# The projections of three head pairs written as one burst each instead of two, with neighbouring operations in another order

## The chip, the cores and the metric

The kernel runs on one core of a Trainium2 chip. The metric is device time in microseconds (us); lower is better. PE is TensorE (matrix multiplies), DVE is VectorE, ACT is ScalarE, POOL is GpSimd, SP is SyncE, which issues the DMAs. "Bank" means a PSUM bank, the 128 x 512 float tile into which matmuls write.

## What is computed

An attention with exponential features over 8 batches and 8 heads of 576 positions and 64 dimensions, and behind it a gated product over the 4608 x 512 result. q, k, v and all weights are drawn at random.

```python
def phi(x):                      # for q and for k, omega is 128 x 64
    proj = np.einsum('bhsd,md->bhsm', x, omega)
    sq = np.sum(x * x, axis=-1, keepdims=True) / 2.0
    h = proj - sq
    h = h - np.max(h, axis=-1, keepdims=True)
    return np.exp(h) / np.sqrt(m)
kv = np.einsum('bhsm,bhsd->bhmd', k_p, v)
z = np.sum(k_p, axis=2)
num = np.einsum('bhsm,bhmd->bhsd', q_p, kv)
den = np.einsum('bhsm,bhm->bhs', q_p, z)[..., None] + 1e-06
x = (num / den)                  # laid out as 4608 x 512
a = x @ w_a                      # 512 x 1536
b = x @ w_b
return (a * b) @ w_out           # 1536 x 512
```

## The kernel before

The work is cut into blocks of 512 rows of x, one batch each (the last 64 positions of all batches make a ninth block). For each block, the attention of four pairs of heads is computed while the PE does the gated product of an earlier block. So PE holds two kinds of work in one stream: the products `pa`, `pb` (x by w_a and w_b, L1307) and `o` (by w_out, L1120), each an instruction group of three 128x512 matmuls (from block 2 on, x by w_a and w_b is done in another form, L1405), and between them the attention of pairs that come later.

The attention of a pair begins with the projection: 64 x 64 matmuls that multiply X (k and q of the pair, eight chunks of 128 positions) by omega into the banks `ppk` and `ppq`. From these, ACT copies the scores into `hk` and `hq` (L396), DVE takes the maximum of each row (a reduce) and works out the bias of the exponentials (two small instructions), and ACT computes the exponentials in place. Then PE multiplies `hk` with v into `pkv` (L906).

Two routines write that projection. `four` (L576) does four chunks into two banks of the ring `at` and is called twice per pair; its scores are handled in `scores` (L632; reduces at L659, biases at L666 and L667, exponentials at L680). `eight` (L593) does all eight chunks in one burst of 64 matmuls (L607) into four banks: two of the ring `at` (`ppk`, `ppq`) and, if it is called with an empty `room`, two of the ring `ab` (`ppkb`, `ppqb`), whose two banks otherwise hold `pa` and `pb`. Its reduces are 1024 wide (L617), its biases stand at L622 and L623, its exponentials at L627. Copies come first on the banks of the second half.

A bank of `ab` that holds `pa` is free when ACT has copied it (a<-pa, L396), one with `pb` when DVE has multiplied it with that copy (a<-pb,a at L1315). The next `pa` or `pb` needs a free bank, and so does `eight`.

Which routine a pair takes is decided in `moe_block`, which starts each step of the gated product with `begin([] if len(steps) >= CFG["OWN"] else None)` (L1294): pairs that start at step 16 or later go to `eight`. The four pairs of the third block (u = 8, 9, 10, 11 in the numbering of `shifted`, L800; their tiles are called `_2_0` to `_2_3`) start at steps 8, 11, 14 and 17, so before the change the first three take `four` twice and the fourth takes `eight`.

Nothing is scheduled at run time. A frozen table, `ORDER`, lists every operation of the program by number; `Graph.plan` replays it, with `SLOTS` (which buffer of its ring each tile takes) and `ENGS` (which of two engines does an operation that either could do). Each engine runs its instructions in that order and waits by semaphores for what they read and for buffers that come free.

In the first 40 us there is hardly any gated product to work on. Block 0's pairs (tiles `_0_0` to `_0_3`) are projected and normalised there, weights are split into two float32r parts, tails of 64 positions (`sme`, `htk`, `htq`, `x32t`, `tails`) are handled, and the squares of k and q (`nat`, on POOL at L750 or ACT at L749) are summed by DVE into `sq` (L752).

Of the kernel before, what the change touches and what calls it, by code (L numbers as in the profile page):

```python
# [40 lines left out]
CFG = dict(EFIRST=0, HALF=1, IDSP=1, EDF=("DVE", "ACT", "POOL"), ROUNDS=2, ZS=800, ZB=(300, 1600, 3600), ZD=(300, 1600, 3100), HQ=(1100, 2600, 3600), BACK2=(300, 1100, 2600), TW=(), XL=["v0", "v1", "Xt0", "ht2", "hq0"], OWR=["raw0", "raw1"], ONE=((7, 1),), SAFE=500, OWN=16, OWNU=(), TG=1, G4=4, WAIT=150, RAW=600, FAST=(0, 1, 2, 3), JOIN0=False, WARM=7, HROOM=["w0", "u1", "w1", "u2", "w2", "u3"], H=3, TURN=(7,), BACK=1500, AT=2, GATES=(-4, -1, 2, 5), SQPE=4, MARGIN=1200, LOAD=1100, SUMS=1000, NATS=(1, 2, 3), CONV=(28000, 2600))  # L41
# [152 lines left out]
"""  # L194

SLOTS = dict(
# [1435 lines left out]
```

## Time and profile before

| what | value |
| --- | --- |
| median of 3 runs | 1031.36 us (1030.74 to 1031.38) |
| the profiled execution | 1031.69 us, of which the span is 1029.7 us |
| PE busy | 1021.7 us, 99% of the span, 9963 matmuls |
| DVE busy | 789.8 us, 77% |
| ACT busy | 637.8 us, 62% |
| POOL busy | 110.8 us, 11% |
| main DMA queue | 87.6% of 16 engines' span |

The span runs from the first to the last instruction of the core; the remaining 2.0 us of the execution lie around it. A matmul's duration overlaps with that of the next, so on PE the distance between the starts of two instructions tells how long one takes, and the end in the row does not. In a timeline a row starts at the first column's time (us from the span's start), and xN counts instructions that were put into one row.

### The profile page before, as it was taken

What the parts mean: (1) busy time and instruction counts of PE and PEld (TensorE: products, weight loads), DVE (VectorE), ACT (ScalarE), POOL (GpSimd) and SP (SyncE); (2) the same over time, 40 slices, a digit from 0 to 9 for tenths busy, and PEclk for the clock granted to TensorE, in tenths of its full rate; (3) what the DMA queues carried; (4) which work ended last, traced back from release to release, by engine and by line L of the source; (5) the groups of instructions that cost most, each with busy time, mean ns of one, the idle gap of its engine ahead of it and who ended that gap; (6) DMA issues with size and microseconds to landing.
All of it is one profiled execution on the core that took longest, in us unless ns stands there. A gap on an engine that the chain in (4) does not pass through costs nothing.

```text
span 1029.7 us, 25658 instructions
## 1 busy us (share of the span) xinstructions
PE 1021.7 (99%) x9963; PEld 900.4 (87%) x9963; DVE 789.8 (77%) x1561; ACT 637.8 (62%) x1688; POOL 110.8 (11%) x182
## 2 busy tenths in 40 slices
PE   9999999999999999999999999999999999999998
PEld 7777777778788889888889988888888999999998
DVE  7999999999987877776767767687756467877555
ACT  7999998776676666675666556675654134344322
POOL 2012111210111111111110011111110000000000
PEclk9999999999999999999999999999999999999999
DMA  9787888998999999989898998989797888989981
GB/s 355 244 308 255 274 257 281 328 320 285 338 338 321 340 350 333 341 299 324 286 341 306 325 290 284 350 273 320 242 331 244 307 281 329 366 319 346 358 310 60
DMA packets 122185, 312.95 MB, mean 304 GB/s; under 512 B 17488, under 2 KB 39120, under 8 KB 122064
## 3 DMA queue, kind: packets, MB, share of 16 engines
q1 hardware_dynamic: 121600, 310.72, 87.6%
q8 instruction: 79, 1.29, 0.5%
q10 hardware_dynamic: 464, 0.59, 0.2%
q14 instruction: 42, 0.34, 0.1%
HBM read 254.74 MB, written 56.52 MB: 302 GB/s over the span
## 4 chain that ended last, share of the span: by engine, by line
PE 96%; DVE 3%; ACT 0%; issue 0%; DVEq 0%; ACTq 0%
PE p L1405 41%; PE o L1120 23%; PE pb L1307 6%; PE pa L1307 6%; PE o_P L1190 5%; PE pkv L906 3%; PE pm L977 2%; PE ppk L607 2%; PE ppk L587 2%; PE p L607 1%; PE p L1190 1%; DVE sm L659 1%; PE ppke L587 1%; DVE raw L456 0%; PE none L426 0%; DVE sq L752 0%
## 5 line engine op out<-in xcount | busy, mean ns | idle before, releaser
L1120 PE MATMUL o<-wo,ghl 128*128 128x512 f32 x1008 | 269.6, 397 | 0.0
L1120 PEld LDWEIGHTS o<-wo,ghl 128*128 128x128 f32 x1008 | 178.6, 188 | 35.5 <-issue 4.3
L396 ACT COPY c<-p 128x512 f32<-128x512 f32 x150 | 87.5, 583 | 182.0 <-PE p L1405 174.4
L1417 DVE TENSOR_TENSOR c<-p,c 128x512 f32<-128x512 f32 x144 | 98.7, 685 | 63.8 <-PE p L1405 36.5
L1405 PE MATMUL p<-Sa,t 128*128 128x256 f32 x1008 | 133.9, 282 | 0.0
L1405 PEld LDWEIGHTS p<-Sa,t 128*128 128x128 f32 x1008 | 126.9, 190 | 2.4 <-issue 0.3
L859 POOL TENSOR_TENSOR z<-hk 128x256 f32<-128x256 f32 x54 | 47.2, 873 | 610.5 <-ACT hk L627 356.1
L1481 DVE TENSOR_TENSOR c<-c 128x512 f32<-128x512 f32 x82 | 56.7, 696 | 46.3 <-ACT c L396 45.7
L1307 PE MATMUL pa<-x,wa 128*128 128x512 f32 x288 | 79.6, 400 | 0.0
L941 ACT ACTIVATE hq<-hq,dn 128x128 f32<-128x128 f32 x216 | 70.5, 393 | 11.9 <-DVE dn L937 11.5
L1307 PE MATMUL pb<-x,wb 128*128 128x512 f32 x288 | 77.8, 397 | 0.0
L1405 PE MATMUL p<-x,wb 128*128 128x256 f32 x504 | 73.5, 281 | 0.0
L1405 PE MATMUL p<-x,wa 128*128 128x256 f32 x504 | 73.4, 281 | 0.0
L1405 PEld LDWEIGHTS p<-x,wa 128*128 128x128 f32 x504 | 67.7, 189 | 2.9
L1405 PE MATMUL p<-Sb,bq 128*128 128x256 f32 x504 | 67.7, 283 | 0.0
L1405 PE MATMUL p<-x,t 128*128 128x256 f32 x504 | 67.5, 282 | 0.0
L1405 PEld LDWEIGHTS p<-Sb,bq 128*128 128x128 f32 x504 | 64.9, 189 | 2.9
L1405 PEld LDWEIGHTS p<-x,t 128*128 128x128 f32 x504 | 64.7, 189 | 2.9
L1405 PE MATMUL p<-Sb,t 128*128 128x256 f32 x504 | 67.0, 282 | 0.0
L1405 PEld LDWEIGHTS p<-x,wb 128*128 128x128 f32 x504 | 65.6, 189 | 0.1
L1405 PEld LDWEIGHTS p<-Sb,t 128*128 128x128 f32 x504 | 63.4, 189 | 1.4 <-ACT c L396 0.5
L1307 PEld LDWEIGHTS pb<-x,wb 128*128 128x128 f32 x288 | 53.3, 188 | 12.7 <-issue 0.9
(225 smaller groups left out, 1969.2 us busy)
## 6 DMA issues: line engine op xcount, KB each, us to landing
t<-td SPq DMA_DIRECT2D x168, 512.0 KB
wo<-wod SPq DMA_DIRECT2D x96, 512.0 KB
bq<-bd SPq DMA_DIRECT2D x84, 256.0 KB
qdr<-qd SPq DMA_DIRECT2D x108, 160.0 KB
hq<-qdr SPq DMA_DIRECT2D x27, 640.0 KB
X<-in_kqt_dram SPq DMA_DIRECT2D x30, 512.0 KB
raw<-in_wab_dram SPq DMA_DIRECT2D x24, 512.0 KB
td<-ts SPq DMA_DIRECT2D x24, 512.0 KB
```

What stands on the lines that cost most here:

```text
L396: nc.scalar.copy(o(), i())
L587: nc.tensor.matmul(pps[w].ap[half, c * M:c * M + M], x()[rows, c * P + D * t:c * P + D * t + D], mo.ap[rows], start=True, stop=True)
L607: nc.tensor.matmul(flat[c // 4][w]()[half, c % 4 * M:c % 4 * M + M], x()[rows, c * P + D * t:c * P + D * t + D], om.ap[rows], start=True, ...
L859: g.op({"POOL": pool2(n)}, lambda e: nc.gpsimd.tensor_tensor(o(), a(), c(), op=ALU.add), r=r, w=w, alloc=list(al), prio=pri, deps=zload[-1 ...
L906: nc.tensor.matmul(pkv.ap[D * j + d:D * j + d + Q, 0:M], vb.ap[:, vc, d:d + Q], c(), start=(n == 0), stop=(n == 4))
L941: g.op({"ACT": 392}, lambda e, c=c, src=src: nc.scalar.activation(hq.ap[:, c], src(), AF.Copy, scale=dn.ap[:, c:c + 1]), r=[sd, (dn, None) ...
L1120: nc.tensor.matmul(po.ap[:], ghl.ap[:, gi, t * P:(t + 1) * P], wo.ap[:, wi], start=(n == 0 and i == 0), stop=(n == NF - 1 and i == 2))
L1190: nc.tensor.matmul(pb.ap[:, t], A[0](ai)[:, t * P:(t + 1) * P], W[0](wi), start=begin and t == j == 0, stop=stop and j == 2 and (t == 1 or ...
L1307: nc.tensor.matmul(pb.ap[:], wt.ap[:, wi, c], xs[c].at(xi), start=(c == 0 and i == 0), stop=(c == NC4 - 1 and i == 2))
L1405: nc.tensor.matmul(pb.ap[:, w], W[w][0](wi, c), X[0](xi, c), start=fresh and n == w == 0, stop=n == 5, skip_group_check=True)
L1417: g.op({"DVE": dve(SM)}, lambda e: nc.vector.tensor_tensor(o.ap[:, q], pb.ap[:], C[y[0]].ap[:, y[1]], op=ALU.add), r=[(pb, 0), (pb, 1), (C ...
L1481: g.op({"DVE": dve(SM)}, lambda e, c=C[k]: nc.vector.tensor_tensor(c.ap[:, :, 1], c.ap[:, :, 1], c.ap[:, :, 0], op=ALU.mult), r=part, w=pa ...
```

## The change

`OWN` goes from 16 to 8, so that the pairs u = 8, 9 and 10 are also projected by `eight` with banks of their own. The graph then has four operations fewer for each of these pairs (5255 instead of 5267 in all), and `ORDER` and `SLOTS` are new tables for it; one letter of `ENGS` differs, by which one copy of an output tile goes from DVE to ACT. The number of PE instructions is the same, and so is SP's stream with its DMAs. DVE has 13 instructions fewer (four for each pair, two reduces of 1024 for four of 512 and two bias instructions for four, and the copy), ACT one more. Rows of the changed kernel carry a line number smaller by one, since a table is one line shorter.

```diff
 CFG = dict(
...
-OWN=16,
+OWN=8,
...
 ORDER = """
-    6 7 3 238 239 9 240 306 307 8 2 360 1 0 241 243 361 242 257 414 311 415 271 256 246 22 245 244 260 258 10 247 259 308 312 250 249 251 261 248 309 264 270 268 314 269 263
...
 SLOTS = dict(
...
-    tst="010212020132a323a93ba323",
+    tst="102012020132a323a93ba323",
...
 ENGS = (
-    "DDDDDDADADADDAADDDPPADDAPADAPPDDADAAAADDDDDADAAAADDADDAADADDAADADADDADDAADDDAADADADDADAADDAAAADADDDDDADADDDAAADADDDDAADDDDDDAAAD")
+    "DDDDDDADADADDAADDDPPADDAPADAPPDDADAAAADDDDAADAAAADDADDAADADDAADADADDADDAADDDAADADADDADAADDAAAADADDDDDADADDDAAADADDDDAADDDDDDAAAD")
```

PE's order is the same up to row 496 of 3137 and again from about row 776; between them the three pairs and the products around them stand differently. On PE at the first of the three pairs (u = 8; `pa0_10` and `pb0_10` are the products of step 10, `o0_2` and the like the output products), before:

```order
L1307 MATMUL pa0_10_2261<-x_0_2_826,wa10_2088 128x512 x3
L587 MATMUL ppk_2_00_2371<-om_67,X_2_0_2208 64x128
...
L587 MATMUL ppq_2_00_2372<-om_67,X_2_0_2208 64x128
L1307 MATMUL pa0_10_2261<-x_0_3_912,wa10_2088 128x512 x3
L1120 MATMUL o0_3_1120<-wo9_2213,ghl0_9_2366 128x512 x3
L1120 MATMUL o0_0_1124<-wo9_2213,ghl0_9_2366 128x512 x3
L1307 MATMUL pb0_10_2340<-x_0_1_734,wb10_2164 128x512 x3
L587 MATMUL ppk_2_04_2433<-om_67,X_2_0_2208 64x128
...
L587 MATMUL ppq_2_04_2434<-om_67,X_2_0_2208 64x128
L1307 MATMUL pb0_10_2340<-x_0_2_826,wb10_2164 128x512 x3
```

and after:

```order
L1306 MATMUL pb0_10_2259<-x_0_3_920,wb10_2192 128x512 x3
L1119 MATMUL o0_2_1205<-wo9_2159,ghl0_9_2339 128x512 x3
L1119 MATMUL o0_0_1114<-wo8_1893,ghl0_8_2162 128x512 x3
L606 MATMUL ppk_2_0_2388<-om_67,X_2_0_2225 64x128
...
L606 MATMUL ppq_2_0_2389<-om_67,X_2_0_2225 64x128
L606 MATMUL ppkb_2_0_2390<-om_67,X_2_0_2225 64x128
...
L606 MATMUL ppqb_2_0_2391<-om_67,X_2_0_2225 64x128
L1119 MATMUL o0_1_1122<-wo8_1893,ghl0_8_2162 128x512 x3
L1119 MATMUL o0_0_1114<-wo9_2159,ghl0_9_2339 128x512 x3
L1306 MATMUL pa0_11_2450<-x_0_0_722,wa11_2365 128x512 x3
```

The two bursts have become one, behind both products of step 10 and two groups of `o`, and two groups of `o` stand between the burst and the next `pa`.

On DVE at the same place, before (`hk`, `hq` are the scores of the pair):

```order
L948 STREAM_TRANSPOSE qd_2182<-hq_1_3_2036 128x4x288
...
L404 TENSOR_TENSOR ghl0_9_2366<-a0_9_2167,ghl0_9_2366 128x512
...
L659 TENSOR_REDUCE sm_2_0_2375<-hk_2_1_2373 128x4
L659 TENSOR_REDUCE sm_2_0_2375<-hq_2_0_2374 128x4
L666 SCALAR_TENSOR_TENSOR sm_2_0_2375<-sm_2_0_2375,sq_2_0_2101 128x2x4
...
L1315 TENSOR_TENSOR a0_10_2262<-pb0_10_2340,a0_10_2262 128x512
L659 TENSOR_REDUCE sm_2_0_2375<-hq_2_0_2374 128x4
```

and after:

```order
L947 STREAM_TRANSPOSE qd_2190<-hq_1_3_2040 128x4x288
L1314 TENSOR_TENSOR a0_10_2275<-pb0_10_2259,a0_10_2275 128x512
...
L616 TENSOR_REDUCE sm_2_0_2394<-hq_2_0_2393 128x8
L616 TENSOR_REDUCE sm_2_0_2394<-hk_2_1_2392 128x8
L621 SCALAR_TENSOR_TENSOR sm_2_0_2394<-sm_2_0_2394,sq_2_0_2114 128x16
```

The multiplication that frees the bank of `pb0_10` now stands right behind the transpose of the pair before, and ahead of both reduces.

On DVE in the first 20 us, before (`sme`: the tails of block 0; `sq_0_1`: the squares of pair 1, summed from `nat_0_1`, which POOL has squared):

```order
L659 TENSOR_REDUCE sme_0_0_273<-ppqe_0_00_270 128x4
L666 SCALAR_TENSOR_TENSOR sme_0_0_273<-sme_0_0_273,pse_0_00_296 128x8
L667 SCALAR_TENSOR_TENSOR sme_0_0_273<-pse_0_00_296,sme_0_0_273 128x8
L752 TENSOR_REDUCE sq_0_1_340<-nat_0_1_148 128x16
L659 TENSOR_REDUCE sm_0_1_244<-ppk_0_14_317 128x4
```

and after:

```order
L658 TENSOR_REDUCE sme_0_0_273<-ppqe_0_00_270 128x4
L751 TENSOR_REDUCE sq_0_1_339<-nat_0_1_151 128x16
L665 SCALAR_TENSOR_TENSOR sme_0_0_273<-sme_0_0_273,pse_0_00_297 128x8
L666 SCALAR_TENSOR_TENSOR sme_0_0_273<-pse_0_00_297,sme_0_0_273 128x8
L658 TENSOR_REDUCE sm_0_1_243<-ppk_0_14_319 128x4
```

The sum of the squares has gone ahead of the two bias instructions of the tails. Further on in the first 60 us, a few neighbours are exchanged on DVE and ACT: two copies `qT_0_1` (L398) go between the reduces of pair 3 and its two bias instructions, and the steps that split the weight tiles `raw1` and `raw2` (L452, L454) go ahead of the copy `x_0_2` on ACT.

## Rows read from the trace of the kernel before

**Rows 1.** The page: busy time by engine, granted clock in 40 slices, chain.

```profile
PE 1021.7 (99%) x9963; PEld 900.4 (87%) x9963; DVE 789.8 (77%) x1561; ACT 637.8 (62%) x1688; POOL 110.8 (11%) x182
PEclk9999999999999999999999999999999999999999
PE 96%; DVE 3%; ACT 0%; issue 0%; DVEq 0%; ACTq 0%
```

**Rows 2.** Waits of PE in the whole span: engine, line, releaser, us, times, longest.

```profile
PE none L426 <- PEq L1616: 0.8, 1, 0.8
...
PE px L1073 <- DVE x32t L1062: 0.4, 1, 0.4
```

**Rows 3.** Busy time in two stretches of 20 us, every engine, granted clock.

```profile
20.00:40.00 20.00, 18.91 (x400) 16.01 (x396) 19.39 (x60) 18.14 (x55) 0.73 (x4) 1.00 0.85 317
...
140.00:160.00 20.00, 20.00 (x188) 15.39 (x187) 17.57 (x36) 19.76 (x55) 2.52 (x4) 1.00 0.76 243
```

**Rows 4.** Timeline of PE around a call of four for u = 9: start, length, instruction.

```profile
167.13 0.84 PE L1307 MATMUL pa<-x,wa 128*128 128x512 f32 x3
167.90 0.32 PE L587 MATMUL ppk<-om,X 64*64 64x128 f32 x1
...
168.94 0.98 PE L1307 MATMUL pb<-x,wb 128*128 128x512 f32 x3
169.75 0.86 PE L1307 MATMUL pa<-x,wa 128*128 128x512 f32 x3
170.45 0.40 PE L1307 MATMUL pb<-x,wb 128*128 128x512 f32 x1
```

**Rows 5.** Timeline of PE around the call of eight for u = 11.

```profile
216.42 0.32 PE L607 MATMUL ppk<-om,X 64*64 64x128 f32 x1
...
217.24 0.27 PE L607 MATMUL ppk<-om,X 64*64 64x128 f32 x1
...
217.35 0.27 PE L607 MATMUL ppkb<-om,X 64*64 64x128 f32 x1
...
218.33 1.68 PE L1120 MATMUL o<-wo,ghl 128*128 128x512 f32 x6
```

**Rows 6.** Timeline of DVE in the first 40 us.

```profile
11.94 0.16 DVE L666 SCALAR_TENSOR_TENSOR sme<-sme,pse 128x8 f32<-128x8 f32 x1
...
12.22 1.22 DVE L752 TENSOR_REDUCE sq<-nat 128x16 f32<-128x1024 f32 x1
13.35 0.68 DVE L659 TENSOR_REDUCE sm<-ppk 128x4 f32<-128x512 f32 x1
...
39.75 0.42 DVE L1062 TENSOR_TENSOR x32t<-pn,rd 128x256 f32<-128x256 f32 x1
```

**Rows 7.** Timelines of POOL and of ACT there, with idle time and its releaser.

```profile
10.01 2.04 POOL L750 TENSOR_TENSOR nat<-nat 128x512 f32<-128x512 f32 x2 [4.88 <-DMA nat<-in_kqn_dram]
...
12.40 0.69 ACT L680 ACTIVATE htk<-ppke,sme 128x128 f32<-128x128 f32 x2
...
15.68 1.40 ACT L680 ACTIVATE hq<-ppq,sm 128x128 f32<-128x128 f32 x5 [0.38 <-DVE sm L673]
...
20.31 0.89 ACT L680 ACTIVATE hq<-ppq,sm 128x128 f32<-128x128 f32 x3 [0.39 <-DVE sm L673]
```

**Rows 8.** Timelines of DVE and ACT around the eight of u = 11.

```profile
213.04 1.38 DVE L948 STREAM_TRANSPOSE qd<-hq 128x1152 f32<-128x1152 f32 x1
...
215.23 0.69 DVE L1315 TENSOR_TENSOR a<-pb,a 128x512 f32<-128x512 f32 x1
...
218.45 0.59 ACT L396 COPY hk<-ppkb 128x512 f32<-128x512 f32 x1 [0.23 <-PE ppqb L607]
...
229.14 0.40 ACT L627 ACTIVATE hk<-hk,sm 128x128 f32<-128x128 f32 x1
```

**Rows 9.** The reduces of both forms: count, ns min/median/max, first and last start.

```profile
L617 DVE TENSOR_REDUCE sm<-hk x20: 1207/1219/1222, 219.1 to 756.1; 128x8 f32<-128x1024 f32 x20
...
L659 DVE TENSOR_REDUCE sm<-hk x6: 676/678/686, 150.3 to 198.6; 128x4 f32<-128x512 f32 x6
```

More of the change, by code (lines that the diff above doesn't have):

```diff
@@ L39 @@
 NS = 2
-CFG = dict(EFIRST=0, HALF=1, IDSP=1, EDF=("DVE", "ACT", "POOL"), ROUNDS=2, ZS=800, ZB=(300, 1600, 3600), ZD=(300, 1600, 3100), HQ=(1100, 2600, 3600), BACK2=(300, 1100, 2600), TW=(), XL=["v0", "v1", "Xt0", "ht2", "hq0"], OWR=["raw0", "raw1"], ONE=((7, 1),), SAFE=500, OWN=16, OWNU=(), TG=1, G4=4, WAIT=150, RAW=600, FAST=(0, 1, 2, 3), JOIN0=False, WARM=7, HROOM=["w0", "u1", "w1", "u2", "w2", "u3"], H=3, TURN=(7,), BACK=1500, AT=2, GATES=(-4, -1, 2, 5), SQPE=4, MARGIN=1200, LOAD=1100, SUMS=1000, NATS=(1, 2, 3), CONV=(28000, 2600))
+CFG = dict(EFIRST=0, HALF=1, IDSP=1, EDF=("DVE", "ACT", "POOL"), ROUNDS=2, ZS=800, ZB=(300, 1600, 3600), ZD=(300, 1600, 3100), HQ=(1100, 2600, 3600), BACK2=(300, 1100, 2600), TW=(), XL=["v0", "v1", "Xt0", "ht2", "hq0"], OWR=["raw0", "raw1"], ONE=((7, 1),), SAFE=500, OWN=8, OWNU=(), TG=1, G4=4, WAIT=150, RAW=600, FAST=(0, 1, 2, 3), JOIN0=False, WARM=7, HROOM=["w0", "u1", "w1", "u2", "w2", "u3"], H=3, TURN=(7,), BACK=1500, AT=2, GATES=(-4, -1, 2, 5), SQPE=4, MARGIN=1200, LOAD=1100, SUMS=1000, NATS=(1, 2, 3), CONV=(28000, 2600))
 ORDER = """
[149 rows of a table removed]
[148 rows of a table added]
 """
@@ L197 @@
     at=(
-        "0123456705613412652106537451673260731742751346507163014510110101010101101010100101011010101001010101101001010101010101010101010110101010101010101010101010010101"
-        "01010101010101010101010101010101010101010101"),
+        "0123456705613412652106537451673260731742751346507163014510110101010101101010100101011001101001101010010101010101010101010110101010101010101010101010010101010101"
+        "01010101010101010101010101010101010101"),
     Xw="01235a",
@@ L208 @@
     ht="0120120120120120",
-    sq="012012102101210210210120121021012012102",
+    tails="00000",
+    sq="012012102101201210210120121021012012102",
     qd="01010000000000000000000000000000",
@@ L212 @@
     nat="010101010101010011010110010011010101010101010101010101010101010",
-    tails="00000",
     rd="1010010101",
@@ L221 @@
     x="01230123012301230110",
-    ab="01010101010101010101010101010101010101010101010101011001",
+    ab="01010101010101010101100101010101010101100101010101010101011001",
     a="101010101010101010101010",
@@ L227 @@
     ghl="010101010101010101010101010101010101010101010101010101010101010101010101010101010101010101010101010101010101",
-    o="0321132032103210321032103210453210241350",
+    o="0321302132103210321032103210453210241350",
     z2="000000000000000000000000000",
@@ L236 @@
     kl="000000000000000000000000000",
-    tst="010212020132a323a93ba323",
+    tst="102012020132a323a93ba323",
     osb="10001010101010",
+    xa="01230123012301",
     t=(
@@ L241 @@
         "12340123"),
-    xa="01230123012301",
     st="00101010101010",
```

296 rows, old and new, of the table ORDER are left out of this document.

## The prediction

> **What bounds the kernel now.** I read the page first. PE is busy 99% of the span, the chain of what ended last lies on PE for 96% and on DVE for 3%, and the granted clock is at its highest digit in every slice [rows 1]. So the kernel takes as long as PE's stream of instructions, and a change can move the time in three ways: PE's instructions take less time, PE waits longer somewhere, or PE waits less. The second view, PE's waits over the whole span, shows how little the third can give: seven waits, the longest 0.8 us [rows 2]. The busy time in stretches tells where they lie: PE is busy 18.91 of the 20 us from 20 to 40, where DVE has 19.39, and 20.00 of 20 between 140 and 160 [rows 3]. So in the first 40 us DVE's row of instructions sets the end, and from there on PE does. The last of these waits, at 40 us, is for the DVE row x32t at 39.75 [rows 2, 6]. What DVE or ACT save behind 60 us is worth nothing by itself; what they cost there is worth nothing until it makes PE wait.
>
> The burst itself is read from PE's timeline by distances between starts. Around a call of four, a plain group of three products takes 0.70 us (169.75 to 170.45). From 167.13 to 169.75 stand one group, the burst of four chunks and one more group: 2.62 us [rows 4]. In steady state one chunk takes 0.11 us (217.24 to 217.35) [rows 5], so four chunks with two halves each make 8 x 0.11 = 0.88, and two plain groups 1.40. What is left, 2.62 - 1.40 - 0.88 = 0.34 us, is the price of going from full matmuls to 64 x 64 ones and back. Within an eight nothing is paid in the middle: its first half takes 0.93 us (216.42 to 217.35), its second 0.98 [rows 5], together 1.91, which is 16 x 0.11 and 0.15 of such edges.
>
> **The change part by part.** *One burst instead of two.* Each of the three pairs goes into and out of the 64 x 64 form once instead of twice: 0.34 us saved for each, 3 x 0.34 = 1.0 us, all of it on PE, which sets the end. Bounds: 0, if a longer burst pays elsewhere what it saves at its edges, and 1.1 (0.36 a pair, if the last digit of each row falls in its favour). I take 1.0, since an eight of this kernel was measured.
>
> *DVE has four instructions fewer for each pair.* Two reduces of 1024 at 1.22 stand for four of 512 at 0.68 [rows 9]: 2.72 - 2.44 = 0.28 us, and of the bias instructions one pair of 0.28 (11.94 to 12.22) [rows 6] is gone. It is 0.5 us a pair of heads, of an engine that PE does not wait for there [rows 2, 3]: worth nothing. The same goes for the copy that moves from DVE to ACT.
>
> *The first 20 us of DVE.* Here DVE sets the end, so an exchange of neighbours counts. The sum sq_0_1 goes ahead of the two bias instructions of the tails. In before it started at 12.22, when POOL's squares had been finished (10.01 + 2.04 = 12.05) for 0.17 us [rows 6, 7]; now it must wait for them. It then starts at about 12.1, and takes its 1.13 us (12.22 to 13.35); the biases, 0.28 (11.94 to 12.22), end at about 13.5 instead of 12.22, and the next reduce starts at about 13.5 where it was 13.35: DVE is later by 0.16. The larger part is ACT's. Its exponentials of the tails, which began at 12.40, begin 1.3 us later. ACT has two places with nothing to do behind that, 0.38 us at 15.68 and 0.39 at 20.31 [rows 7], which swallow 0.77; 0.53 us are left over. ACT hands back the banks whose scores DVE reduces next, so some of that reaches DVE. Against it stands the other exchange: with the copies between them, the two bias instructions of pair 3 no longer follow each other at once. A dependent pair of this kind takes 0.28 us for two short instructions [rows 6]; I put down 0.13 for the gap that closes. Net +0.4 (0.53 - 0.13). Bounds: -0.13, if nothing of ACT's delay arrives, and +1.3, if all of it does. I take +0.4, nearest to the row with the idle time that ACT has. Of the exchanged weight steps on ACT nothing is on the path: PE's last wait in this stretch is for DVE.
>
> *The middle, 145 to 210 us.* PE has no idle time there, so a gain is excluded; a loss is a new wait at one of three points. First, the second half of eight needs the bank of pb0_10, that is the end of the multiplication. From the last matmul of pb0_10 to the second half stand two groups of o (1.40) and the first half (0.93): 2.3 us. At u = 11 the multiplication started at 215.23 and took 0.69, and the second half began at 217.35 [rows 5, 8]: 1.4 us to spare. Second, pa0_11 follows two groups (1.40) behind the end of eight and needs the bank of ppkb copied by ACT; at u = 11 this copy started 0.12 us behind the end of the burst (218.33) and took 0.59 [rows 5, 8]: 0.7 to spare. At u = 8 ACT is fuller (19.76 of 20 us) [rows 3], so less. Third, pkv needs the exponentials of hk. In the changed order 17 groups stand between eight and pkv, 17 x 0.70 and the burst of 1.91 plus edges: 14.0 us. At u = 11 the last exponential of hk ended 229.14 + 0.40 - 216.42 = 13.1 us behind the start of the burst [rows 5, 8]: 0.9 to spare, again with an ACT that had less to do. I take +0.1 for all three pairs; bounds 0 and 1.5 (0.5 for each pair: one transpose of 1.4 more ahead, less the 0.9 that u = 11 had to spare).
>
> *The sum.* -1.0 + 0.4 + 0.1 = -0.5 us. On the profiled execution, 1031.69, that is 1031.2; the profiled one is 0.33 above the median of 1031.36, so on the median it is 1030.9. SP's stream is unchanged, so its queue moves with the buffers, by less than a microsecond.
>
> A measurement of this kernel can tell about 0.2% from no change, 2.06 us: 1029.3 to 1033.4 is "the same".
>
> **The rivals.** *The start loses all.* If the delay of 1.3 us on ACT reaches DVE whole, the sum is -1.0 + 1.3 + 0.1 = +0.4: 1031.8. For it: DVE has no gap there (19.39 of 20). Against: the two idle places on ACT [rows 3, 7]. Chance 0.17.
>
> *The bank of pb holds the burst up (slower).* In the changed order the multiplication stands right behind the transpose of qd, which took 1.38 us at u = 11 [rows 8] and itself reads what ACT finishes last for the pair before. From the point where the multiplication ends later than 2.3 us after pb's last matmul, every microsecond is one of PE. At u = 11 it ended at 215.92, 1.4 us ahead of the second half [rows 5, 8], so one such transpose ahead uses that up and no more; a transpose that itself waits as long again for ACT makes 1.38 us a pair. If all three pairs pay it, 4.1 - 1.0 + 0.4 = +3.5: 1034.9; if one does, +0.8: 1032.2. For it: the order on DVE. Against: only u = 8 has this neighbourhood for certain. Chance of all three 0.04, of one 0.10.
>
> *The copies are the bound.* A burst fills four banks that ACT alone empties, 0.59 us each [rows 8]; if other work of ACT stands between these copies, pa0_11 waits. At u = 8 ACT's stream from its copy of pa0_10 to that of ppkb has six long instructions and three short ones, some 4 us at 0.59 for a long one, where PE has four groups, the burst and two groups (4 x 0.70 + 1.91 + 1.40 = 6.1) between the two points. It decides from where ACT runs more than 2 us behind PE; what ACT had to spare at u = 11, 0.7 a pair, is the price if it is lost twice over, 2.1 in all, and 2.1 - 1.0 + 0.4 = +1.5: 1032.9. The Trainium skill ("TensorEngine Tiling (Array Packing)", PSUM Bottleneck) states this as the rule: tiling speeds up TensorE but not the emptying of PSUM, so the copy may become the bottleneck; it advises to share the copies between ScalarE and VectorE, which this kernel does not do for these banks. By that rule the time would be the 1032.9 of this rival. The trace so far disagrees, with 0.7 us to spare at u = 11. Chance 0.09.
>
> *The burst does not do what it says.* If the edges of a burst are paid for its length, the 1.0 is not saved: +0.5, 1031.9. The timeline of u = 11 speaks against it [rows 5]. Chance 0.05.
>
> **How the numbers follow.** The forecast, 1030.9, with a start between -0.13 and +0.8, has 0.55: 1030.2 to 1031.3. The cases up to 1032.9 have 0.17, 0.10, 0.09 and 0.05, the slow one 0.04. A range from 1030.0 to 1032.6 leaves out less than 2 in 10: the slow case and most of the copies' case above, and a few in a hundred below. Faster by over 0.2% would need 1029.3, more than twice what the burst gives: 0.03. Slower by over 0.2%: the slow case, and what a row of mishaps adds: 0.07. The same: 0.90.
>
> **What would show it.** The changed profile should have no 64 x 64 burst of 16 pairs of matmuls for u = 8 to 10, three more bursts with a 0.11 step into ppkb, and edges of 0.15 and not twice that. PE's total of waits should stay below 4 us, all of it before 60 us; the x32t that PE waits for at 40 us should come 0.2 to 0.8 later than 39.75. Step one is wrong if a burst has a gap between its halves. The middle is wrong if a wait of PE appears on ppkb behind a multiplication, on pa behind a copy, or on pkv behind an exponential. The forecast as a whole is wrong if the start moves by more than 1 us in either direction.

## The result: 1.3% slower, with the profile after

The changed kernel takes 1046.17 us (median of 6 runs, 1041.29 to 1048.18) against 1031.37 us of the kernel before beside it, 14.8 us more. The ratio estimated from all runs is 1.0132, 95% interval 1.012 to 1.0143 (the medians alone give 1.014). The forecast had been 1030.9, with a range up to 1032.6. The profiled execution took 1042.26 us, with a span of 1040.4.

The page after: busy time, and the chain that ended last.

```profile
PE 1020.7 (98%) x9963; PEld 899.5 (86%) x9963; DVE 786.6 (76%) x1548; ACT 638.1 (61%) x1689; POOL 109.0 (10%) x182
...
PE 75%; DVE 0%; ACT 0%; issue 0%
```

PE is busy 1.0 us less than before [rows 1], which is the saving that the edges of the bursts should give, and the span is 10.7 us longer. So the loss is waiting. PE's waits in the whole span after (us in total, times, longest):

```profile
PE pa L1306 <- ACT hk L395: 3.5, 2, 2.5
PE pkv L905 <- ACT hk L626: 2.9, 2, 1.7
PE pm L976 <- ACT kl L395: 1.4, 1, 1.4
...
PE px L1072 <- DVE x32t L1061: 0.8, 1, 0.8
```

The first three kinds were not there before [rows 2]. Stretches of 20 us after (length, then busy time of PE, PEld, DVE, ACT and POOL, clock, DMA share, GB/s) show where they lie:

```profile
20.00:40.00 20.00, 18.51 (x390) 15.61 (x388) 19.04 (x59) 19.41 (x58) 0.60 (x3) 1.00 0.85 318
...
140.00:160.00 20.00, 19.04 (x210) 14.63 (x210) 15.95 (x29) 16.63 (x42) 3.04 (x4) 1.00 0.70 256
...
220.00:240.00 20.00, 17.46 (x157) 13.62 (x156) 16.98 (x33) 13.81 (x37) 0.16 (x1) 1.00 0.90 323
```

Before, PE had no idle moment from 140 to 260 us ([rows 3] has the first 20 of them); now it is idle for 8.4 of these 120 us. ACT and DVE are busy for less of them as well (90 and 103 us, before 96 and 110). A row of PE that is the same in both traces comes 1.4 us later at 63 to 131 us and 10.6 us later at 244 us; behind that the distance stays between 10.0 and 10.6. The timeline of PE after, with the first burst and the waits:

```profile
152.04 0.32 PE L606 MATMUL ppk<-om,X 64*64 64x128 f32 x1
...
152.96 0.27 PE L606 MATMUL ppkb<-om,X 64*64 64x128 f32 x1
...
153.94 1.67 PE L1119 MATMUL o<-wo,ghl 128*128 128x512 f32 x6
156.57 1.65 PE L1306 MATMUL pa<-x,wa 128*128 128x512 f32 x6 [0.96 <-ACT hk L395]
...
168.29 1.08 PE L905 MATMUL pkv<-hk,v 128*32 128x128 f32 x32 [1.18 <-ACT hk L626]
...
190.85 0.96 PE L905 MATMUL pkv<-hk,v 128*32 128x128 f32 x26 [1.68 <-ACT hk L626]
191.76 0.60 PE L976 MATMUL pm<-hq,kl 128*32 128x512 f32 x2
...
214.25 1.07 PE L976 MATMUL pm<-hq,kl 128*32 128x512 f32 x8 [1.44 <-ACT kl L395]
```

The burst has no gap between its halves and takes the forecast 1.9 us. Behind it PE waits for the copies of its banks (156.57) and for the exponentials (168.29). The same follows the later bursts: pkv waits 1.68 at 190.85, pm 1.44 at 214.25, and pa 2.54 at 228.05, behind the fourth burst, which was there before. What ACT and DVE did meanwhile, first DVE and then ACT:

```profile
152.73 0.43 DVE L874 STREAM_TRANSPOSE z<-zs 128x256 f32<-128x256 f32 x1
...
157.52 1.22 DVE L616 TENSOR_REDUCE sm<-hq 128x8 f32<-128x1024 f32 x1 [1.24 <-ACT hq L395]
...
163.44 0.28 DVE L924 CUSTOM_DVE_ANT_0 zero<-htq,zb 64x128 bf16<-64x128 f32 x1 [1.95 <-DMA zb<-zdr]
```

```profile
153.42 0.63 ACT L565 ACTIVATE natq<-natq 128x512 f32<-128x512 f32 x1 [0.72 <-DMA natq<-in_kqn_dram]
...
155.93 0.59 ACT L395 COPY hk<-ppkb 128x512 f32<-128x512 f32 x1
...
160.38 0.41 ACT L626 ACTIVATE hq<-hq,sm 128x128 f32<-128x128 f32 x1
...
164.80 0.66 ACT L395 CAST wo<-raw 128x512 fp32r<-128x512 f32 x1 [0.94 <-DVE raw L455]
...
190.89 0.30 ACT L395 COPY kl<-hq 128x128 f32<-128x128 f32 x1
...
213.90 0.30 ACT L395 COPY kl<-hq 128x128 f32<-128x128 f32 x1 [2.13 <-DMA hq<-qdr]
...
225.34 0.63 ACT L565 ACTIVATE natk<-natk 128x512 f32<-128x512 f32 x1 [3.90 <-DMA natk<-in_kqn_dram]
```

Four of PE's six waits can be followed back here (not the 1.68, nor a 0.62 at 250.63). ACT, which works in order, stands 0.72 us for the data of a square ahead of the copies that `pa` needs. DVE stands 1.95 us for `zb`, the sums z of the keys of the step before, which the division needs and which make a trip through DRAM (stored as `zdr`, fetched as `zb`). The conversion of `raw` behind that is late, ACT waits 0.94 for it, and the exponentials queued behind on ACT come 1.18 too late for `pkv`. At 213.90 `kl` stands 2.13 for the queries that come back from DRAM, and `pm` waits for it. At 225.34 a square holds up the copies of the fourth burst by 3.90.

### The profile page after: what moved, and what is told of

Same layout as the page of the kernel before. It is cut to its first block, busy times and chain, and to the rows that moved or that the text cites. A ratio compares the mean times of both kernels' runs of the same rounds, so it can differ in the third digit from the quotient of the medians.

```text
span 1040.4 us, 25637 instructions
## 1 busy us (share of the span) xinstructions
PE 1020.7 (98%) x9963; PEld 899.5 (86%) x9963; DVE 786.6 (76%) x1548; ACT 638.1 (61%) x1689; POOL 109.0 (10%) x182
## 4 chain that ended last, share of the span: by engine, by line
PE 75%; DVE 0%; ACT 0%; issue 0%
PE p L1404 41%; PE o L1119 18%; PE o_P L1189 5%; PE pkv L905 2%; PE pm L976 2%; PE ppk L606 2%; PE p L606 1%; PE pb L1306 1%; PE pa L1306 1%; PE p L1189 1%; PE ppke L586 0%; PE pkv L978 0%; PE ppq L606 0%; DVE oe L1253 0%; PE ppkb L606 0%; PE ppk L586 0%
## 5 line engine op out<-in xcount | busy, mean ns | idle before, releaser
L626 ACT ACTIVATE hk<-hk,sm 128x128 f32<-128x128 f32 x184 | 60.1, 391 | 13.2 <-DVE sm L622 13.2
L1306 PEld LDWEIGHTS pa<-x,wa 128*128 128x128 f32 x288 | 52.9, 188 | 17.2 <-ACT hk L395 4.6
```

The source lines that it names most:

```text
L626: g.op({"ACT": 392}, lambda e, c=c, w=w, to=to, at=at: nc.scalar.activation(to.ap[:, at + c], to.ap[:, at + c], AF.Exp, scale=SC, bias=sm. ...
L1306: nc.tensor.matmul(pb.ap[:], wt.ap[:, wi, c], xs[c].at(xi), start=(c == 0 and i == 0), stop=(c == NC4 - 1 and i == 2))
```

## What a burst does to the pair's row of steps

The timelines of before show the same steps for u = 8 when the pair was projected in two fours (PE, ACT and DVE rows):

```profile
147.93 0.32 PE L587 MATMUL ppk<-om,X 64*64 64x128 f32 x1
...
162.74 1.08 PE L906 MATMUL pkv<-hk,v 128*32 128x128 f32 x32
...
187.38 1.04 PE L977 MATMUL pm<-hq,kl 128*32 128x512 f32 x8
```

```profile
152.07 0.41 ACT L680 ACTIVATE hq<-hq,sm 128x128 f32<-128x128 f32 x1
...
182.52 0.29 ACT L396 COPY kl<-hq 128x128 f32<-128x128 f32 x1
```

```profile
143.84 0.43 DVE L875 STREAM_TRANSPOSE z<-zs 128x256 f32<-128x256 f32 x1
```

Before, the first half of the scores was projected 4.0 us ahead of the second (147.93 and 151.92), and its exponentials began at 152.07, while the second four ran. After, all sixteen begin at 160.38 or later, though the burst stands at 152.04: the first exponential comes 8.3 us behind the first projection instead of 4.1. At u = 9 and 10 this distance grows less, from 5.9 to 6.1 and from 5.4 to 7.4.

Three more steps hang on the exponentials: the sum z, its trip through DRAM, and the division, the transposing and a second trip of the queries (`qdr`, `hq`) up to `kl` and `pm`. To follow one pair one has to know which rows are its own: step u projects the queries of pair u and the keys of pair u + 1 (`hq_2_0` and `hk_2_1` in the orders of u = 8). The keys go into the `pkv` of the same step, the queries into the `pm` beside the `pkv` of the next. Starts subtracted, in us, with what PE waited in between in brackets (before nothing):

| from, to | before u = 8, 9, 10 | after u = 8, 9, 10 |
| --- | --- | --- |
| first projection to the pkv of its keys | 14.8, 18.4, 13.6 | 16.3 (2.1), 15.3 (1.7), 12.5 (0) |
| first projection to the pm of its queries | 39.5, 40.3, 39.2 | 39.7 (3.8), 38.7 (3.1), 43.6 (4.0) |
| kl of these queries to that pm | 4.9, 3.6, 3.3 | 0.9, 0.4, 2.8 |

The first projections stand at 147.93, 167.90 and 193.51 before and at 152.04, 175.54 and 198.80 after, these pm rows at 187.38, 208.20 and 232.72 before and at 191.76, 214.25 and 242.41 after. Without PE's waits the way from projection to pm is 35.9, 35.6 and 39.6 us long after: 3.6 and 4.7 less than before at u = 8 and 9, and 0.4 more at u = 10. Of the 4.9 and 3.6 us that kl was ahead of pm (it takes 0.3 itself), 0.9 and 0.4 are left; at u = 10 it is 2.8 of 3.3, and that pm does not wait. On the way, the z that divides the queries of u = 8 starts late by the new order (POOL had its sum at 147.39, DVE turned to it at 152.73); for the queries of u = 9, DVE waits for POOL and POOL for the exponentials.

## Experiments

Each run gives its median in us and, in brackets, its ratio to the kernel before run beside it, with the 95% interval.

**Where it is lost: start or middle.** `e2`: the kernel before with the first 786 operations in the changed order. `e1`: the changed kernel with those 786 in the old order. `e5`: all operations ahead of the first burst in the old order.

```diff
 ORDER = """
-(operations 1 to 786 of the one kernel)
+(operations 1 to 786 of the other)
```

> The kernel before (two bursts for each of the three pairs), with its first 786 operations in the changed order. Theory A expects 1.4 us more than before, about 1032.8, and no stall of PE behind 110 us. Theory B expects stalls of PE between 140 and 260 us and over 1036.

> The changed kernel, with its first 786 operations (up to about 110 us, before the first of the three bursts) in the order of the kernel before; the rest as changed. Theory A (the start costs only what its own trace shows: the same PE rows stand 1.39 us later from 63 us on) expects the changed kernel's time less 1.4 us, with the stalls of PE between 140 and 260 us still there (8 us and more). Theory B (the new order of the start is what makes the middle late) expects the stalls gone and about 1031.

> The changed kernel (one burst for each of the three pairs), with all operations that stand ahead of the first of the three bursts in the order of the kernel before, and what follows in the changed order. The theory that the loads are late because of the order of the 30 us ahead of the first burst expects most of the loss gone: the stalls at the first burst and at the pkv behind it disappear, and the time is 1031 to 1035. The theory that the changed order behind the first burst is too tight by itself (or the burst is) expects stalls of 5 us and more still there, 1037 to 1042.

`e2` 1033.14 (1.0015, 1.0006 to 1.0024): the start costs 1.6 us. `e1` 1043.22 (1.0107, 1.0092 to 1.0122): the rest costs the larger part. `e5` 1039.82 (1.0072, 1.0056 to 1.0089), with 6.1 us of idle PE between 140 and 260: some 8 us remain when the changed order begins only at the burst.

**The burst or the new order.** `e6` puts the three bursts into the old order, moving only what must move; `e7` puts in the burst of u = 8 alone, `e8` that of u = 10 alone.

```diff
-            begin([] if len(steps) >= CFG["OWN"] else None)
+            begin([] if len(steps) in (8, 17) or len(steps) >= CFG["OWN"] else None)
```

(This is `e7`; `e8` has 14 in place of 8.)

> The kernel before in its own order, with the two bursts of each of the three pairs made one, put behind the products whose banks it needs; copies, reduces, biases and exponentials stand where those of the second burst stood, and the exponentials of the first half between them. So the burst is changed and nothing else is reordered on purpose. The theory that the burst itself is the loss (four banks emptied by ACT alone, scores later by half a pair) expects PE to wait for copies, multiplications or exponentials at all three pairs, 1036 or more. The theory that the loss lies in the new order expects 1029.5 to 1033: 1.0 us gained at the edges, and waits of about 0.5 us a pair at most.

> The kernel before in its own order, with one burst for the first of the three pairs (u = 8) alone, placed as in the run of the bursts in the old order; the other two pairs keep two bursts. In the kernel before ACT is busy 19.76 of the 20 us in which this pair is projected. The theory that the loss comes from ACT standing still while it waits for the scores, in a stretch in which it has no time to spare, expects most of the 7.7 us of the three bursts here: 4 us or more, 1035 to 1038. A theory in which each burst costs about the same expects a third, +2.6 us, 1034.

> The same with one burst for the third of the three pairs (u = 10) alone, where ACT is busy 14.18 of 20 us in the kernel before. The theory of ACT without time to spare expects no loss: 1031.0 to 1032.0 (the 0.34 us of one edge gained, and a short wait). The theory of the same price for each burst expects +2.6 us, 1034.

`e6` 1039.62 (1.0072, 1.0055 to 1.0088), `e7` 1033.63 (1.0023, 1.0014 to 1.0033), `e8` 1034.07 (1.0027, 1.0016 to 1.0038). One burst costs 2.3 to 2.7 us, edges saved included, and three cost 7.7, three times as much. So the burst costs this in the old order too. There it stands where the second four stood, at u = 8 right ahead of the `pa` that needs its banks; another place was not tried. PE's longest wait in `e7`, and PE in `e8`, behind the one burst:

```profile
PE pa L1308 <- ACT hk L397: 1.8, 1, 1.8
```

```profile
199.06 1.67 PE L1308 MATMUL pa<-x,wa 128*128 128x512 f32 x6 [0.74 <-ACT hk L397]
...
207.64 1.65 PE L1308 MATMUL pa<-x,wa 128*128 128x512 f32 x6 [0.65 <-ACT a L397]
...
212.10 1.67 PE L1308 MATMUL pb<-x,wb 128*128 128x512 f32 x6 [0.62 <-DVE a L1316]
```

In `e8` the waits are for other things than in the changed kernel (there pkv and pm too, here only the products' banks), 2.0 us together; in `e7` pkv waits 0.7 beside the 1.8 of pa. So in the old order most of the price is that of banks that are not yet empty.

**Late loads.** `e3`: the changed kernel with the sum of one `natq` on DVE back at its old place, since SP's next load waits for it (131.84 before, 137.85 after). `e4`: that with the old start. `e9`: the other way round, the sum 10 places later in the kernel before. `e10`: the changed kernel with shorter output stores in block 0, which leaves the rest of that block's output unwritten.

```diff
 DVE
-8 instructions, TENSOR_REDUCE sq<-natq
+TENSOR_REDUCE sq<-natq, the same 8 instructions
```

> The changed kernel with one DVE instruction, the sum of the squares of natq of pair u = 8, put back to where it stood before (8 places earlier on DVE, right behind the split of wo). SP's load of the next natq, and all loads queued behind it, wait for that sum. The theory of the late loads (SP held up by DVE, squares and weight steps on ACT late, bank copies queued behind them) expects 2 to 6 us less than the changed kernel. The theory of the burst (four banks that ACT alone empties) expects no change, within 0.5 us.

> Both of the above: the start of the kernel before and the one sum early. The theory of the late loads expects the sum of both gains, 3.4 us or more below the changed kernel; the theory of the burst expects 1.4.

> The kernel before, with one DVE instruction moved: the sum of the squares of natq of pair u = 8 stands 10 instructions later, as about in the changed order, so that SP issues the load behind it, and all loads after that, some 4 us later. No burst is changed. The theory of the late loads as a cause by themselves expects stalls of PE behind 145 us and 1033 or more. If a late load can be made up for as long as nothing else is late, the time stays within 0.5 us of the kernel before.

```diff
-dma(lambda: out[b * S + t * P:b * S + (t + 1) * P, :], lambda: osb.ap[:, h])
+dma(lambda: out[b * S + t * P:b * S + t * P + (8 if b == 0 else P), :], lambda: osb.ap[0:8 if b == 0 else P, h])
```

> The changed kernel with the four stores of the first block's rows (at about 185 to 191 us) cut to 8 rows of 128 each; the rest of that block's output is left unwritten. It takes about 1 MB from the DMA engines, some 3 us at the 300 GB/s that the changed kernel moves there, at a time when they are busy 94% and the kernel is late. The theory that lost time cannot be made up because the DMA engines have none to spare expects about 2 to 3 us less than the changed kernel. The theory that ACT and DVE in their fixed order set the pace expects no change, within 1 us.

`e3` 1044.85 (1.0121, 1.0103 to 1.014): pa's wait at 156 falls from 0.96 to 0.24, but pkv's grows to 2.9. `e4` 1041.68 (1.011, 1.0084 to 1.0135). `e9` 1031.31 (1.000, 0.999 to 1.001): one late load costs the old kernel nothing. It came 4.4 us late there (136.26), but from 143 us on SP's loads were within 0.5 us of their old times, and in `e3` the loads behind the early one stayed as late as in the changed kernel (`raw` at 140.04, there 139.94). So a queue that is late as a whole was not tried by itself. `e10` 1042.86 (1.0112, 1.0097 to 1.0127), within the changed kernel's own runs: not settled. The changed kernel run again, `e11`, gave 1044.87 (1.0133, 1.0117 to 1.0149).

> The changed kernel again, on the same chip as the next three, to have its own time beside theirs. Expected: 1041 to 1048, and in a profile of an execution over 1044 at least two falls of the granted clock to half, each behind a wait of PE of 2 us or more.

The two falls came, at waits of 2.15 and 2.44 us, and a third at 13.9 us behind a wait of 1.59.

**The copies.** `e12`: in the changed kernel the banks `ppkb` and `ppqb` of all four bursts are copied by DVE, right behind the burst. `e13`: the three squares that stand ahead of the copies on ACT go behind them. `e14`: both, and the old start.

```diff
-                g.op({"ACT": act(4 * M)}, copier(lambda to=to, at=at, i=i: to.ap[:, at + 4 * i:at + 4 * i + 4],
+                g.op({"DVE": dve(4 * M)} if i and b == 2 else {"ACT": act(4 * M)}, copier(lambda to=to, at=at, i=i: to.ap[:, at + 4 * i:at + 4 * i + 4],
```

> The changed kernel with the two copies of the second half of each burst (the banks that pa and pb need next) on DVE instead of ACT, right behind the burst. The theory of the banks (a burst takes both banks of pa and pb, and PE has nothing but o to do until they are copied) expects the waits of pa for a copy (0.96 and 2.54 us in the profile of the changed kernel) gone, and with them the falls of the clock that follow: 3 to 6 us less than the changed kernel. The theory that the late loads hold everything up expects the stalls to move to pkv, and less than 1.5 us gained.

> The changed kernel with three ACT instructions (the squares of natq and natk that stand ahead of the copies of the bursts at u = 8, 10 and 11, and wait for their loads) moved behind the copies. No engine changes. The theory of the banks expects about the same gain as with the copies on DVE, most at u = 11, where ACT waited 3.90 us for natk: 2 to 5 us less than the changed kernel. The theory that the scores of the next pair are the bound expects less than 1 us.

> The start in the order of before, the copies of the second halves on DVE, and the three squares behind the copies. If the start (1.6), the banks and the clock that falls behind long waits are the whole of the loss, 1031 to 1034. If 3 us or more are left over, the scores that come later for a whole pair (pkv waiting for exponentials) are a cause of their own.

`e12` 1048.2 (1.0163, 1.0148 to 1.0178), `e13` 1043.87 (1.0127, 1.011 to 1.0144), `e14` 1047.0 (1.0153, 1.0136 to 1.017). PE's waits in `e12`:

```profile
PE pb L1308 <- DVE a L1316: 4.3, 2, 3.5
PE pkv L907 <- ACT hk L628: 4.1, 2, 2.1
PE pa L1308 <- ACT a L397: 2.5, 1, 2.5
```

The wait of pa for the copies of hk is gone, as meant, and DVE's multiplications are late instead: 3.3 us slower than the changed kernel beside it (`e11`), 2.0 slower than in the result. The Trainium skill ("TensorEngine Tiling (Array Packing)", PSUM Bottleneck) advises to share such copies between ScalarE and VectorE; here the run went the other way. In `e13` the same wait is gone too, and pkv waits 3.5 and pb 2.3; the 1.0 us to `e11` is within the runs of either. In `e14` pkv (3.8), pb (3.1) and pa (2.6) wait.

**Has DVE no time to spare?** DVE is busy 92% between 140 and 260 us before, so I took it that what it stands still around a burst is never made up. `e15`: the weight sums `wr` on POOL instead of DVE; `e16`: the same in the kernel before, the control; `e17`: the changed kernel with pkv four groups later, which gives the pair's exponentials 2.8 us more.

```diff
-            g.op({"DVE": dve(SM)}, lambda e, k=k, v=v: ENG[e].tensor_tensor(wr.ap[:, k], v(0), v(1), op=ALU.add),
+            g.op({"POOL": dve(SM)}, lambda e, k=k, v=v: ENG[e].tensor_tensor(wr.ap[:, k], v(0), v(1), op=ALU.add),
```

> The changed kernel, with the sums of two weight tiles (wr, 128 x 512, 0.68 us each on DVE, 16 of them between 140 and 260 us, 10.9 us) done by POOL instead of DVE. Theory that DVE has no time to spare there, so that what a burst makes it stand still is never made up: between 140 and 260 us PE's idle time falls from 8.4 us to under 4, and the time from some 1044.5 to 1037 to 1041. Theory that each burst has a chain of its own that is too long, whatever DVE has to do beside it: idle time of PE within 1.5 us of 8.4, time within 2 us of the changed kernel's. POOL's own sums may take longer than DVE's and delay the weights' transfers, which would show as waits on DMA.

> The kernel before, with the same sums on POOL instead of DVE: the control. PE has no wait between 140 and 260 us to lose, so both theories expect the time of the kernel before, 1031.4, within 0.5 us; a longer time would be the price of the sums on POOL themselves, to be taken off what the same move does to the changed kernel.

> The changed kernel, with the multiplication of hk with v (pkv) of the pairs u = 8, 9 and 10 put behind the four groups of the gated product that follow it, 2.8 us later on PE. Theory that each burst's own chain is too long: pkv's waits for the exponentials of hk (1.18 and 1.68 us) go and nothing comes in their place, so the time falls by about 3 us. Theory that DVE has no time to spare: the waits of pkv go, and most of them come back at the products or the transposed queries behind, so that the time falls by less than 1.5 us or rises.

`e15` 1049.06 (1.0173, 1.0153 to 1.0193), `e16` 1032.0 (1.0006, 0.9996 to 1.0015), `e17` 1053.01 (1.0195, 1.0172 to 1.0219). Both came out against the theory that they were made for. In `e15` PE is idle 12.2 us instead of 8.4 between 140 and 260, with DVE busy 93 us instead of 103. A row of DVE there:

```profile
167.55 0.28 DVE L924 CUSTOM_DVE_ANT_0 zero<-htq,zb 64x128 bf16<-64x128 f32 x1 [4.03 <-DMA zb<-zdr]
```

DVE waits for `zb` longer than in the changed kernel (1.95). So 10 us less work on DVE gained nothing, and at this point DVE is short of data, not of time. (A sum takes POOL some 1.3 us and DVE 0.68, so a part of the loss may be theirs; the control, within 1 us of the kernel before, bounds it only where there is slack.) In `e17` pkv no longer waits for hk, but pb waits 12.0 us for DVE:

```profile
172.82 3.87 PE L1308 MATMUL pb<-x,wb 128*128 128x512 f32 x9 [4.44 <-DVE a L1316]
```

The same group of PE instructions multiplies the earlier pair's queries (`pm`), from which the next rows of x come; four groups later for pkv is four groups later for those, and the copies of both on ACT and DVE moved with them. The run thus did not give the pair more time alone, and can't speak for the theory of the long chain.

**All named waits at once.** `e18`: the changed kernel with the squares of `e13`, and:

```diff
 DVE, u = 8
-zero<-htq,zb x2, raw<-raw, wr<-wa x2
+raw<-raw, wr<-wa x2, zero<-htq,zb x2
 SP, u = 9 and 10
-zdr<-zx, ..., qdr<-qd x4, zb<-zdr
+zdr<-zx, zb<-zdr, ..., qdr<-qd x4
 ACT, u = 9
-osb<-o, hk<-hk, osb<-o, hk<-hk x2
+hk<-hk x3, osb<-o, osb<-o
```

> The changed kernel with one exchange of neighbours for each wait of PE between 150 and 230 us whose cause its trace names: the three squares on ACT go behind the burst's copies (e13); DVE divides by the fetched denominators (zb, which it waited 1.95 us for) behind three instructions that are ready, at u = 8; the load of zb follows its store at once on SP at u = 9 and 10, not behind the stores of the transposed queries; three exponentials of hk go ahead of two copies of o that wait for PE, at u = 9. Theory that a pair's chain (scores, exponentials, sums, two trips through DRAM) has become too long for its place and stalls an in-order engine at a few known points: PE's idle time between 140 and 260 us falls from 8.4 us to 4 or less, no long wait is left, and the time falls from some 1044.9 to 1035 to 1039. Theory that an engine has no time to spare, or that the banks are the limit: other waits take their place, PE's idle time stays at 7 or more and the time within 2 us of the changed kernel's.

`e18` 1045.33 (1.0139, 1.0121 to 1.0156): no gain. PE's waits, and ACT and DVE at u = 9:

```profile
PE pm L978 <- ACT kl L397: 4.8, 2, 2.8
PE pkv L907 <- ACT hk L628: 1.7, 1, 1.7
```

```profile
191.95 0.30 ACT L397 COPY kl<-hq 128x128 f32<-128x128 f32 x1 [3.84 <-DMA hq<-qdr]
```

```profile
183.88 0.28 DVE L926 CUSTOM_DVE_ANT_0 zero<-htq,zb 64x128 bf16<-64x128 f32 x1
...
186.78 1.23 DVE L930 TENSOR_TENSOR qd<-hq,zb 128x1024 f32<-128x1024 f32 x1 [1.60 <-DMA qdr<-qd]
```

The waits of pa, and DVE's long waits for zb, are gone (one of 0.63 is left). In their place PE waits 4.8 us for `kl`, the end of the second trip: the load of zb now goes ahead of the stores of the queries on SP (`zb` at 179.41, the first `qdr` at 180.30, where it was 178.68), and hq is fetched at 186.73 where it was 184.49. Both trips share SP's queue, and what one gains there the other loses. PE is idle 6.9 us instead of 8.4.

## Why the prediction was wrong, point by point

*The edges: right.* PE is busy 1.0 us less, and the halves follow at once.

*The start: right in kind, wrong in size.* Forecast +0.4 with a bound of +1.3; `e2` measured +1.6. The two idle places of ACT were to swallow 0.77 of the 1.3. The DVE row x32t at 39.75 came 0.65 us later, as forecast (0.2 to 0.8), but by 63 us all PE rows were 1.4 later: over half of it arises behind 40 us, from exchanges that were not priced at all. The wait for x32t in [rows 2] is not at 40 us either, as the prediction has it, but ahead of PE's row at 35.27; the row behind the x32t of 39.75 shows none:

```profile
35.27 0.63 PE L1073 MATMUL px<-ident,x32t 128*128 128x128 f32 x4 [0.36 <-DVE x32t L1062]
...
40.23 0.66 PE L1073 MATMUL px<-ident,x32t 128*128 128x128 f32 x4
```

*The middle: wrong, and it decides.* Forecast +0.1 with a bound of 1.5; PE waits 8.4 us there, and three bursts alone cost 7.7 (`e6`). Two of the three signs that were to show it came: waits of pa behind a copy and of pkv behind an exponential. The step that failed is the sentence on three points, each measured at u = 11 and carried over. For pkv it said 14.0 us of room against 13.1 needed. The room was right (16.3 less 2.1 waited is 14.1 at u = 8, 15.3 less 1.7 is 13.6 at u = 9), but the need was 16.3 and 15.3; only at u = 10, without a wait in 12.5, it was as small as at u = 11. For `pa` behind the copies, 0.7 to spare became a wait of 0.96 at u = 8, where the square stands ahead. And three points were too few: the trips through DRAM, whose spare time at the end (3.3 to 4.9 us from kl to pm, before) rows of before would have shown, are in no term of the sum, and `pm` waits 1.44 behind them.

*The rivals.* The bank of pb as a block between the halves did not come: there is no gap. The copies as the bound had the place of two of the waits (0.96 and 2.54) and of the longest in `e7` (1.8), but the price was too small (2.1 in all), and the cure that it points to made it worse (`e12`). The time lay above all of them.

*The cause, as far as it is settled.* Shown: the loss is waiting of PE, 8.4 us of it between 140 and 260; a burst costs 2.3 to 2.7 us in the old order as well (`e6` to `e8`); at u = 8 the first exponential comes 8.3 us behind the first projection instead of 4.1; 10 us less work on DVE win nothing (`e15`); where a named wait is removed, PE waits elsewhere and hardly any time is won (`e3`, `e13`, `e18`). Argued from this, and not shown: the banks cost a part, as in `e7` and `e8`, and in the changed order a pair's row of steps, from the first projection through two trips through DRAM to its pm, got 3.6 and 4.7 us less of PE's time at u = 8 and 9, where kl had been 4.9 and 3.6 us ahead. Which of the two weighs more is open. Open too: whether another place of the burst, or more steps of the gated product for each pair, would win the 3 x 0.34 us after all. No run moved a whole pair, and `e17`, meant to, moved other work too. No run beat the kernel before.

## What the runs showed of the clock

Late in some of its waits or behind them the granted clock of PE falls to its lower level, 0.50 of full speed, that is 1.2 GHz. PE in `e6`, and the stretches of 2 us there:

```profile
187.26 1.72 PE L1121 MATMUL o<-wo,ghl 128*128 128x512 f32 x6 [2.16 <-ACT osb L397]
188.78 1.48 PE L1308 MATMUL pb<-x,wb 128*128 128x512 f32 x3
190.06 1.48 PE L1308 MATMUL pa<-x,wa 128*128 128x512 f32 x3
```

```profile
186.00:188.00 2.00, 0.74 (x3) 0.65 (x4) 1.97 (x2) 2.00 (x6) 1.35 (x2) 1.00 0.69 270
188.00:190.00 2.00, 2.00 (x7) 1.57 (x7) 1.36 (x5) 0.89 (x3) 1.77 (x5) 0.67 0.78 292
190.00:192.00 2.00, 2.00 (x6) 1.55 (x5) 1.93 (x6) 0.32 (x1) 0.31 (x1) 0.50 0.15 52
```

Groups of three take 1.28 us there (188.78 to 190.06) instead of 0.70, and 2 x 0.33 + 2 x 0.50 = 1.7 us are lost on top of the wait. It also fell at waits of 2.19 (`e1`), 2.90 (`e3`), 2.77 and 2.06 (`e18`) and 1.59 (`e11`, at 13.9 us), and not at 2.54 in the profile after, 2.40 (`e4`) or 2.70 (`e1`): the length of the wait alone does not tell. In the six executions of the result, those with a mean clock of 0.998 or 0.999 took 1041 to 1042 us, those with 0.996 or 0.997 some 1046 to 1048; in the four of `e11` the clock does not sort them (1045.26 at 0.998, 1042.75 at 0.997). By estimate, two such falls (2 x 1.7) are 3.4 us of the 4.2 between the profiled execution's 10.6 and the median's 14.8; of the result only the execution of 1042.26 was profiled, and it has no fall. A price of 1.7 for a long wait stood nowhere in my sum.

## What to carry to other kernels

An engine that is always busy says nothing of what the work beside it has to spare. Before two bursts become one, follow one tile's steps by name to the last user, transfers included (the user beside it in time may be another pair's), and subtract the starts: what the first half comes later is paid from the smallest spare time on that row and, once that is gone, by the bound engine. A distance measured at one pair (here u = 11) holds for another only if the queues around it hold the same.
